# Ten instead of eight of the twelve d_ff blocks of tokens 768 to 1535 in seven-product steps, with a newly searched instruction order

## The chip, the core and the metric

The kernel runs on one NeuronCore of a Trainium2 chip. Its engines are TensorE (PE in the rows; PEld is its weight load), VectorE (DVE), ScalarE (ACT), GpSimd (POOL) and SyncE (SP), which issues every transfer here. The metric is the device time of one execution in microseconds.

## The reference

```python
# attention: B, H, S, D = 4, 8, 576, 64
scores = scale * q @ k.T ; causal mask ; a = softmax(scores)
local = a @ v
q_p = phi(q)                                   # elu(q) + 1
mem_out = (q_p @ M_prev) / (q_p . z_prev + 1e-6)
attn = g * mem_out + (1 - g) * local           # g = sigmoid(beta), one per head
x = attn.transpose(0, 2, 1, 3).reshape(2304, 512)
# gated MLP: w_a, w_b are 512 x 1536, w_out is 1536 x 512
out = (x @ w_a) * (x @ w_b) @ w_out
```

All is in float32, the MLP's weights arrive as float64. The kernel makes a product of two float32 matrices from three matmuls of float32r halves: high by high, high by low, low by high.

## The kernel before

**Stages.** The attention runs first, in sixteen pairs of heads, and fills the first 205 us; its outputs go to DRAM. Then comes the MLP. The 2304 tokens are six blocks of 384 (t = 0 to 5), d_ff is twelve blocks of 128 (f = 0 to 11). The weights are turned from float64 to two float32r halves while the MLP already runs, one block after another, by ScalarE, GpSimd and VectorE.

**Columns.** For t = 0 and 1 each (t, f) is a *column*: `half` makes a and b (12 matmuls of 384 token columns each, line 1027), `product` multiplies and splits them (ScalarE lines 1040 and 1047, VectorE lines 1043 and 300), `outer` adds the result times w_out to three output banks (9 matmuls of 512 columns, line 1064). There are 24 such columns. For t = 2 and 3 the blocks f from FA upward, here 8 to 11, are columns too, eight of them. The list `columns` is in lines 1501 to 1503.

**Seven-product steps.** The rest is done two token blocks at a time, by a scheme that needs seven 256 by 128 by 384 products where the two columns of a plain method need eight. A step n is one f for a pair of token blocks: n = 0 to 7 are f = 0 to 7 for t = 2 and 3 (group 0), n = 8 to 19 are all twelve f for t = 4 and 5 (group 1). A step

- loads the raw float32 weights of its f from DRAM into one of two buffers (`raw_load`, SyncE, line 1339), forms four differences of them on GpSimd (`raw_sums`, line 1354), and splits these (ScalarE line 1357, VectorE line 300);
- loads three ready split quarters (`whole_load`, line 1346);
- makes seven products of six matmuls (`part`, line 1381), with four copies on ScalarE (line 1396) and four joins on VectorE (line 1402) among them;
- splits the two hidden halves (lines 1417, 1419 and 300) and adds four rows of the output at once (`row`, 3 matmuls of 512 columns each, line 1433). Two more rows of each step are left for later: their split halves are kept in SBUF, at the place that `kept` gives, and `late_row` multiplies them once the group is over.

Before a group starts, its token blocks must be summed in eight pieces and split (VectorE line 1300, ScalarE line 1309).

**Memory units.** Tokens of t = 2 to 5 get their memory part in sixteen *units* (`memory_unit`), four for each t. A unit loads its q by four transfers of 48 KB (or eight of 24 KB), into one of two buffers; ScalarE's two exponentials of it (line 1182, 1183) wait for these transfers, VectorE normalises and turns it (the split of the turned tile, written `yl`, is the last reader of the buffer), TensorE multiplies it (line 1257), VectorE adds it to the attention's part.

**The order.** Each engine executes its instructions strictly in the order of one flat list, ORDER, of some 2900 names; BANKS gives the PSUM bank of each tile of the attention. A wait at the head of an engine's queue holds everything behind it.

Of the kernel before, what the change touches and what calls it, by code (L numbers as in the profile page):

```python
# [26 lines left out]
e4.0 e2A.1 lo1.0 m2B.1 r_.0 S_.1 n2.0 ma.2 H1.1 thq.2 m3B.1 m3A.1 mB.1 S_4.1 tlq.2 mb.2 n4.0 G5.0
Lk.3 mA.1 high1.1 G2B.0 n0.0 Lt.3 TQ.2 e2B.1 mx.0 e3B.1 n1.0 n3.0 e3A.1 shift2.0 ga.0 h2B.0 G4.0
m4.1 h5.0 G0.0 TK.2 eA.1 G3A.0 Lv.2 G1.0 l5.0 lo0.1 Lk.4 thQ.2 h4.0 h0.0 thK.2 h3A.0 w_0.0 eB.1
l2B.0 G2A.0 lo0.2 h2A.0 tlQ.2 clamp2.0 high1.2 low1.0 mu.2 G3B.0 l0.0 h3B.0 l4.0 e4.1 h1.0 b_3.2  # L30
tlK.2 S_3.2 TQ.3 thQ.3 Tq.3 l3A.0 shift2.1 l2A.0 l3B.0 TK.3 V1A.0 v_h.1 low1.1 m3A.2 l1.0 r_.1 thK.3
tlQ.3 e3A.2 V2A.0 ma.3 v_l.1 thq.3 b_2.2 xA.0 sq.4 tlK.3 mag0.2 n2.1 high2.1 S_2.2 mc.2 m3B.2 e3B.2
m2B.2 b_.2 mb.3 high1.3 S_.2 V1B.0 V2B.0 m2A.2 G2A.1 e2B.2 G2B.1 Lk.5 n4.1 mag1.4 n1.1 mB.2 tlq.3
e2A.2 G1.1 eB.2 clamp2.1 xB.0 md.2 h2A.1 mA.2 h2B.1 h1.1 n3.1 eA.2 n0.1 mu.3 l2A.1 S_4.2 mc.3 Lv.3
G0.1 G3B.1 m4.2 low2.2 l2B.1 h3B.1 G4.1 h0.1 v_h.2 TQ.4 l1.1 H1.2 h4.1 l3B.1 w_0.1 G3A.1 lo0.3 b_3.3
l4.1 h3A.1 shift0.1 shift0.2 e4.2 S_3.3 l3A.1 G5.1 r_.2 Lt.4 m3A.3 TK.4 l0.1 ma.4 h5.1 V1A.1 l5.1
thQ.4 v_l.2 m3B.3 lo1.1 V2A.1 thK.4 mag2.0 b_2.3 clamp1.1 tlK.4 tlQ.4 shift2.2 e3A.3 Lv.4 S_2.3
m2B.3 b_.3 m2A.3 n2.2 S_.3 sq.5 e3B.3 H0.0 n0.2 n1.2 mB.3 n3.2 xA.1 st_.0 e2B.3 mb.4 n4.2 e2A.3
V1B.1 high0.2 G0.2 eB.3 V2B.1 h0.2 clamp2.2 hi0.1 mag0.3 G2B.2 G2A.2 G5.2 xB.1 low2.3 h2A.2 Tq.4
G1.2 mA.3 w_0.2 mag0.4 h2B.2 md.3 mu.4 l2A.2 h1.2 S_4.3 l0.2 v_h.3 h5.2 G3B.2 thq.4 sq.6 G4.2 G3A.2  # L40
shift0.3 hl.0 b_3.4 l2B.2 l1.2 v_l.3 clamp2.3 l5.2 Lk.6 eA.3 S_3.4 h4.2 TK.5 tlq.4 me.2 m4.3 mag2.1
l4.2 hi1.0 TQ.5 shift1.3 hh.0 h3B.2 l3B.2 h3A.2 l3A.2 e4.3 mc.4 r_.3 V1A.2 thQ.5 m3A.4 n0.3 n4.3
Lt.5 b_2.4 tlQ.5 cx.1 m3B.4 thK.5 V2A.2 S_2.4 n2.3 Tq.5 n1.3 b_.4 lo0.4 tlK.5 S_.4 e3A.4 G0.3 ma.5
V1B.2 V2B.2 cx.2 xA.2 m2B.4 m2A.4 mb.5 e3B.4 hh.1 G2A.3 LM.2 thq.5 st_.1 G1.3 e2B.4 e2A.4 low1.2
high0.3 G5.3 G4.3 Lt.6 H0.1 h0.3 G2B.3 n3.3 lo1.2 mB.4 mA.4 eB.4 mag2.2 S_4.4 xB.2 tlq.5 h2A.3 H0.2
mu.5 TQ.6 shift0.4 h1.3 v_h.4 md.4 hl.1 high2.2 l2A.3 h5.3 G3A.3 h2B.3 b_3.5 h4.3 w_0.3 l0.3 l1.3
lo1.3 S_3.5 G3B.3 l5.3 v_l.4 eA.4 l2B.3 m4.4 h3A.3 TK.6 l4.3 V1A.3 e4.4 thQ.6 clamp1.2 mag2.3 mc.5
low0.2 mx.1 h3B.3 lo1.4 l3A.3 V2A.3 m3A.5 b_2.5 thK.6 r_.4 ma.6 me.3 e3A.5 low1.3 tlQ.6 n1.4 S_2.5
m3B.5 tlK.6 e3B.5 sq.7 b_.5 low0.3 hi1.1 l3B.3 S_.5 m2B.5 n0.4 mb.6 Tq.6 mB.5 hi0.2 n2.4 st_.2 Lt.7
# [1630 lines left out]
```

## Time and profile before

| | us |
|---|---|
| three runs | 652.19, 652.51, 655.13 (median 652.51) |
| the profiled execution, its own time | 654.46 |
| its span, first to last instruction | 652.7 |
| PE busy | 637.8 |
| DVE busy | 485.1 |
| ACT busy | 390.9 |
| POOL busy | 288.1 |

The time is 1.8 us more than the span. An engine is busy while an instruction of it executes; matmuls overlap in the record, so what the next costs is read from where it starts, not from its duration. The attention ends near 205 us, columns fill the time to about 400 us, seven-product steps the rest.

### The profile page before, as it was taken

The numbers are of one execution on the slowest core, as the hardware profiler recorded it, in microseconds if no ns is written. First come the engines' busy times: TensorE is split into PE (matmuls) and PEld (weight loads), VectorE is DVE, ScalarE is ACT, GpSimd is POOL, SyncE is SP. The second block draws the span as 40 slices with busy tenths as digits, with TensorE's granted clock in tenths as the row PEclk, the third lists the DMA queues.
The fourth block names the chain that finished last, engine by engine and source line by source line (L and its number), as shares of the span: only waits on it lengthen the run. The fifth ranks groups of instructions, "written<-read, shape, count | busy, mean of one in ns | idle before, by whom it ended". The sixth has DMA issues, their size and how long they took to land.

```text
span 652.7 us, 11644 instructions
## 1 busy us (share of the span) xinstructions
PE 637.8 (98%) x3962; PEld 586.1 (90%) x3962; DVE 485.1 (74%) x911; ACT 390.9 (60%) x941; POOL 288.1 (44%) x418
## 2 busy tenths in 40 slices
PE   8899999999999999999999999999989999999998
PEld 6788889999889899988999999999988999999987
DVE  7999998998889888889767679687758543545330
ACT  6999999999887445534555556556545433344220
POOL 4999999999995111461000006244140413233000
PEclk9999999999999999999999999999989999999999
DMA  7966776484763889987434436355733344525101
GB/s 175 197 138 166 189 155 168 121 190 136 231 202 138 281 280 323 313 273 267 125 69 97 113 107 202 102 155 172 219 74 113 129 125 149 166 93 161 49 33 64
DMA packets 142314, 105.43 MB, mean 162 GB/s; under 512 B 100272, under 2 KB 121776, under 8 KB 142256
## 3 DMA queue, kind: packets, MB, share of 16 engines
q1 hardware_dynamic: 142256, 104.70, 55.8%
q8 instruction: 31, 0.51, 0.3%
q14 instruction: 27, 0.22, 0.1%
HBM read 74.78 MB, written 29.88 MB: 160 GB/s over the span
## 4 chain that ended last, share of the span: by engine, by line
PE 71%; DVE 10%; DMA 5%; POOL 4%; ACT 4%; issue 2%; SPq 2%; ACTq 0%; DVEq 0%; POOLq 0%
PE pp L1381 20%; PE pp L1027 11%; PE pt L296 7%; PE o L1064 6%; PE o L1433 6%; PE pw L810 6%; PE pt L644 5%; PE pr L1433 4%; PE m L1433 2%; DVE wt L979 2%; DVE wt L986 1%; POOL P L710 1%; PE pw L644 1%; DMA q<-in_q_dram 1%; ACT P L693 1%
## 5 line engine op out<-in xcount | busy, mean ns | idle before, releaser
L1354 POOL TENSOR_TENSOR raw<-raw 128x256 f32<-128x256 f32 x80 | 67.3, 843 | 218.1 <-DMA raw<-ws 127.2
L710 POOL TENSOR_SCALAR P<-P,sum 128x128 f32<-128x128 f32 (+4 forms) x144 | 81.5, 587 | 2.5 <-DVE sum L702 2.2
L693 ACT ACTIVATE P<-pt,nm 128x384 f32<-128x384 f32 (+3 forms) x128 | 66.9, 535 | 2.8 <-DVE nm L683 1.4
L300 DVE TENSOR_TENSOR PT<-pt,PT 128x512 fp32r<-128x512 f32 (+2 forms) x112 | 61.8, 586 | 4.0 <-ACT PT L765 2.9
L810 PE MATMUL pw<-PT,vh 128*128 128x448 f32 (+4 forms) x352 | 61.0, 316 | 0.4 <-ACT xo L819 0.3
L683 DVE TENSOR_REDUCE nm<-pt 128x1 f32<-128x128 f32 (+3 forms) x128 | 56.3, 480 | 4.6 <-PE pt L644 3.9
L810 PEld LDWEIGHTS pw<-PT,vh 128*128 128x128 f32 x352 | 54.9, 189 | 4.5 <-ACT xo L819 0.6
L296 PE MATMUL pt<-ident,P 128*128 128x128 f32 (+1 forms) x400 | 55.2, 277 | 1.3 <-POOL P L710 0.7
L1027 PE MATMUL pp<-xh,abh 128*128 128x384 f32 x160 | 53.9, 337 | 1.6 <-ACT x L1040 1.0
L765 ACT ACTIVATE PT<-pt 128x512 fp32r<-128x512 f32 (+2 forms) x112 | 53.3, 527 | 3.5 <-PE pw L810 2.0
L1027 PE MATMUL pp<-xh,abl 128*128 128x384 f32 x160 | 53.8, 336 | 0.0
L1027 PE MATMUL pp<-xl,abh 128*128 128x384 f32 x160 | 53.6, 335 | 0.0
L965 POOL TENSOR_SCALAR wt<-wt 128x512 f32<-128x512 f32 (+1 forms) x21 | 19.9, 949 | 66.9 <-ACT wt L959 66.8
L296 PEld LDWEIGHTS pt<-ident,P 128*128 128x128 f32 (+1 forms) x400 | 44.1, 140 | 5.2 <-POOL P L710 1.6
L1402 DVE TENSOR_TENSOR u<-pp,u 128x384 f32<-128x384 f32 x40 | 22.2, 555 | 35.0 <-PE pp L1381 28.3
L1381 PE MATMUL pp<-xh,abh 128*128 128x384 f32 x112 | 37.7, 336 | 1.9 <-ACT h L1396 1.9
L1381 PE MATMUL pp<-xh,abl 128*128 128x384 f32 x112 | 37.9, 339 | 0.0
L1064 PE MATMUL o<-wh,hl 128*128 128x512 f32 x96 | 37.8, 394 | 0.0
L1381 PE MATMUL pp<-xl,abh 128*128 128x384 f32 x112 | 37.8, 337 | 0.0
L1064 PE MATMUL o<-wl,hh 128*128 128x512 f32 x96 | 37.8, 393 | 0.0
L1064 PE MATMUL o<-wh,hh 128*128 128x512 f32 x96 | 37.4, 389 | 0.0
L959 ACT ACTIVATE wt<-wr 128x1024 f32<-128x1024 f32 (+1 forms) x24 | 22.0, 917 | 23.9 <-DMA ws<-wt 9.7
(248 smaller groups left out, 1925.6 us busy)
## 6 DMA issues: line engine op xcount, KB each, us to landing
raw<-ws SPq DMA_DIRECT2D x20, 512.0 KB, 4.4
xs<-xo SPq DMA_DIRECT2D x16, 576.0 KB, 4.4
abh<-wsa SPq DMA_DIRECT2D x18, 384.0 KB, 3.4
abl<-wsa SPq DMA_DIRECT2D x18, 384.0 KB, 4.2
wr<-in_moe_w_a_dram SPq DMA_DIRECT2D x12, 512.0 KB, 5.3
wr<-in_moe_w_b_dram SPq DMA_DIRECT2D x12, 512.0 KB, 6.1
wr<-in_moe_w_out_dram SPq DMA_DIRECT2D x12, 512.0 KB, 4.4
ws<-wt SPq DMA_DIRECT2D x12, 512.0 KB, 3.1
```

What stands on the lines that cost most here:

```text
L296: nc.tensor.transpose(out, x, ident[0:x.shape[0], 0:x.shape[0]])
L300: eng.tensor_tensor(out=lo, in0=x, in1=hi, op=ALU.subtract)
L683: nc.vector.tensor_reduce(out=s["nm"][:, c:c + 1], in_=src, axis=AX.X, op=ALU.min)
L693: nc.scalar.activation(out=s["P", i][:, h, :], in_=src, func=AF.Exp, scale=-1.0, bias=s["nm"][:, c:c + 1], accum_out=s["sums"][:, c, 0:1],)
L710: nc.gpsimd.tensor_scalar(out=pr[:, h, :], in0=pr[:, h, :], scalar1=r[:, c:c + 1], scalar2=1.0, op0=ALU.mult, op1=ALU.mult,)
L765: nc.scalar.activation(out=dst, in_=src, func=AF.Copy)
L810: nc.tensor.matmul(pv[:, a:hi], lhsT=w, rhs=x, start=(n == 0), stop=(n == len(ops) - 1))
L1027: nc.tensor.matmul(pp, lhsT=w[:, w0:w0 + P], rhs=x[:, kk, :], start=(c == 0), stop=(c == 3 * KK - 1),)
L1064: nc.tensor.matmul(po[t, m], lhsT=hx[:, m * P:(m + 1) * P], rhs=w, start=(f == START_F[t] and n == 0), stop=(f == NFT - 1 and n == 2 and t ...
L1354: nc.gpsimd.tensor_tensor(out=o, in0=x, in1=y, op=op)
L1381: nc.tensor.matmul(r[nm], lhsT=a[:, kk * P:(kk + 1) * P], rhs=b[:, kk, :], start=first and c == 0, stop=True, skip_group_check=True,)
L1433: nc.tensor.matmul(o, lhsT=hx[:, a:a + P], rhs=z, start=bool(first and i == 0), stop=last and i == 2, skip_group_check=True,)
```

## The change

FA goes from 8 to 10. Blocks f = 8 and 9 of t = 2 and 3 leave the columns (28 instead of 32 remain) and become two more steps of group 0, which has ten steps then; group 1 follows as n = 10 to 21. `kept` gets a place for the kept halves of the two new steps: the fourth quarter of the two regions into which `whole_load` writes, where group 1 keeps its own first two. ORDER and BANKS are replaced as a whole, in the attention too.

```diff
 ORDER = """
-Dk.0 id.0 Dq.0 zi.0 ib.0 clamp1.0 ms.0 wm.14 TK.0 low2.0 Dk.1 mk.0 thK.0 TQ.0 b_2.0 thQ.0 Dq.1 zq.0
...
+id.0 high0.1 zi.0 wm.14 low2.0 Dk.0 TK.0 mag0.2 Dq.0 thK.0 Dk.1 mk.0 zq.0 TQ.0 Ek.0 high1.0 thQ.0 Dq.1
...
-    FA = 8
+    FA = 10
     START_F = {0: 0, 1: 0, NB: FA, NB + 1: FA}
...
                 return [x.rearrange("p k c -> p (k c)")[:, (f - 2) * Q:(f - 1) * Q] for x in xhl[1]]
+        elif f > 7 and not g:
+            a = W6 * (f - 6) + 3 * Q
         else:
             a = W6 * 4 + (f - 4 * g) * Q
```

**ScalarE, the last memory unit.** `ph<-q` and `ph<-ph` are the exponentials of a unit, `n<-n` and `yh<-q` belong to the units too; `u`, `h` and `pp` out of `pp` are the copies of a step, `hh` and `abh` out of `u` or `h` its splits, `abh<-raw` the split of its weight differences. Before:

```order
L1419 ACTIVATE abh<-h_6507 128x256
L1247 ACTIVATE m<-xx 128x384
L1396 ACTIVATE u_6609<-pp 128x384
L1417 ACTIVATE hh<-u_6540 128x384
L1182 ACTIVATE ph<-q_6626 128x384
L1183 ACTIVATE ph<-ph 128x384
L1396 ACTIVATE h_6640<-pp 128x384
L1396 ACTIVATE u_6642<-pp 128x384
```

Now:

```order
L1361 ACTIVATE abh<-raw_4391 128x1024
L1214 ACTIVATE n_6472<-n_6470 32x12 x4
L1421 ACTIVATE hh<-h_6427 128x128
L1423 ACTIVATE abh<-h_6427 128x256
L1400 ACTIVATE u_6533<-pp 128x384
L1400 ACTIVATE h_6544<-pp 128x384
L1421 ACTIVATE hh<-u_6438 128x384
L1400 ACTIVATE u_6574<-pp 128x384
L1242 ACTIVATE yh<-q_6347 128x384
L1184 ACTIVATE ph<-q_6507 128x384
L1185 ACTIVATE ph<-ph 128x384
L1400 ACTIVATE pp<-pp 128x384
```

Behind the unit's exponentials two copies of a step stood before; now the split of another unit and three copies have moved ahead of them, and the copy right behind is that of the next step.

**SyncE, the transfers around the last load of q.** `abh` and `abl` out of `wsa` are the split quarters, `raw` out of `ws` the raw weights. Before:

```order
L1339 DMA raw_4391<-ws_61 128x1024
L1346 DMA abh<-wsa_80 128x768
L1346 DMA abl<-wsa_80 128x768
L1157 DMA q_6626<-in_q_dram 32x12x32 x4
L1176 DMA xf<-xs 64x384
```

Now:

```order
L1343 DMA raw_4392<-ws_70 128x1024
L1350 DMA abh<-wsa_81 128x768
L1350 DMA abl<-wsa_81 128x768
L1159 DMA q_6507<-in_q_dram 32x12x32 x4
L1178 DMA xf<-xs 64x384
```

The load stands behind the same kinds of transfers as before; they now belong to the two blocks that have become steps.

**VectorE, the pieces ahead of the first step.** `pc...` out of `xf` and `xl` out of `xf` are splits of the eight pieces, `xf<-xf` their sums, `x` and `hl` belong to columns. Before:

```order
L1078 COPY raw_4391<-o_5475 128x512
L300 TENSOR_TENSOR pcT1l<-xf,pcT1h 128x768
L1300 TENSOR_TENSOR xf<-xf 128x768 x2
L1218 TENSOR_TENSOR n_5624<-n_5623,n_5625 128x12
L1221 TENSOR_SCALAR n_5624<-n_5624,over_gate_91 128x12
L1225 RECIPROCAL n_5624<-n_5624 128x12
L1043 TENSOR_TENSOR x<-pp,x 128x384
L1230 TENSOR_TENSOR ph<-ph,n_5624 128x384
L1300 TENSOR_TENSOR xf<-xf 128x768
```

Now:

```order
L302 TENSOR_TENSOR xl_98<-xf,xh_97 128x768
L302 TENSOR_TENSOR pcT1l<-xf,pcT1h 128x768
L1302 TENSOR_TENSOR xf<-xf 128x768 x3
L302 TENSOR_TENSOR pcTT2l<-xf,pcTT2h 128x768
L302 TENSOR_TENSOR pcT4l<-xf,pcT4h 128x768
L1045 TENSOR_TENSOR x<-pp,x 128x384
L1206 TENSOR_REDUCE n_5614<-q_5441 128x12
```

The sums and splits, which stood between parts of columns and units, now stand together.

## Rows read from the trace of the kernel before

**Rows 1.** The page, busy time of each engine.
```profile
PE 637.8 (98%) x3962; PEld 586.1 (90%) x3962; DVE 485.1 (74%) x911; ACT 390.9 (60%) x941; POOL 288.1 (44%) x418
```

**Rows 2.** Stretches: us; busy of PE, PEld, DVE, ACT, POOL (x instructions); clock; DMA.
```profile
0.00:50.00 50.00, 46.07 (x362) 38.27 (x363) 44.51 (x103) 42.85 (x123) 39.67 (x68) 1.00 0.80 174
...
100.00:150.00 50.00, 50.00 (x429) 45.86 (x429) 44.41 (x97) 47.35 (x137) 48.52 (x83) 1.00 0.66 158
150.00:200.00 50.00, 47.95 (x391) 42.88 (x389) 42.83 (x88) 44.01 (x119) 47.39 (x74) 1.00 0.58 180
200.00:250.00 50.00, 48.74 (x264) 45.83 (x263) 44.04 (x59) 24.96 (x38) 11.28 (x12) 1.00 0.75 255
250.00:300.00 50.00, 47.80 (x251) 44.07 (x250) 43.34 (x54) 23.52 (x35) 19.83 (x22) 1.00 0.92 294
...
350.00:400.00 50.00, 50.00 (x269) 47.35 (x268) 39.12 (x75) 28.43 (x64) 4.40 (x6) 1.00 0.46 132
...
450.00:500.00 50.00, 48.13 (x245) 44.43 (x244) 36.62 (x70) 25.96 (x58) 12.79 (x15) 0.97 0.44 117
```

**Rows 3.** Waits of PE, whole span: total us, times, longest us.
```profile
PE pp L1027 <- ACT x L1040: 2.4, 3, 1.0
...
PE pp L1381 <- ACT h L1396: 1.9, 1, 1.9
...
PE pp L1027 <- DVE x L1043: 1.1, 2, 0.6
```

**Rows 4.** Chain and ACT's timeline near 478 us: start, us, what [idle before].
```profile
471.92 5.72 DMA q<-in_q_dram
...
477.74 0.52 ACT L1182 ACTIVATE ph<-q 128x384 f32<-128x384 f32 x1 [3.69 <-DMA q<-in_q_dram]
...
478.73 0.48 ACT h L1396
479.25 1.59 PE pp L1381 x6
```

**Rows 5.** PE's timeline behind that stop: start us, us, instruction [idle before].
```profile
479.25 0.44 PE L1381 MATMUL pp<-xh,abh 128*128 128x384 f32 x1 [1.87 <-ACT h L1396]
...
480.64 0.63 PE L1433 MATMUL o<-wh,hh 128*128 128x512 f32 x1
481.06 0.63 PE L1433 MATMUL o<-wl,hh 128*128 128x512 f32 x1
...
484.41 0.39 PE L1433 MATMUL o<-wh,hh 128*128 128x512 f32 x1
```

**Rows 6.** Transfers into q, from issue to landing.
```profile
DMA to landing us min/median/max: 1.6/2.2/6.5
```

**Rows 7.** Runs of matmuls in the chain: start us, us, what.
```profile
318.95 8.34 PE pp L1027 x48
...
510.00 4.18 PE pp L1381 x24
...
631.28 8.17 PE pr L1433 x36
```

**Rows 8.** Groups by shape, 205 to 640 us (POOL: whole span): busy us, mean ns.
```profile
L300 DVE TENSOR_TENSOR abl<-raw,abh 128x1024 fp32r<-128x1024 f32 x20 | 25.8, 1289 | 7.6 <-ACT abh L1357 7.6
L1402 DVE TENSOR_TENSOR u<-pp,u 128x384 f32<-128x384 f32 x40 | 22.2, 555 | 35.0 <-PE pp L1381 28.3 <-ACT u L1396 6.7
L300 DVE TENSOR_TENSOR hl<-x,hh 128x384 fp32r<-128x384 f32 x31 | 20.0, 644 | 3.7 <-ACT hh L1047 2.9
L1043 DVE TENSOR_TENSOR x<-pp,x 128x384 f32<-128x384 f32 x31 | 17.1, 550 | 10.8 <-ACT x L1040 6.3 <-PE pp L1027 4.1 <-ACT pcT3h L1309 0.5
...
L300 DVE TENSOR_TENSOR hl<-u,hh 128x128 fp32r<-128x128 f32 x12 | 3.5, 290 | 3.2 <-ACT hh L1417 3.2
...
L1354 POOL TENSOR_TENSOR raw<-raw 128x256 f32<-128x256 f32 x80 | 67.3, 843 | 218.1 <-DMA raw<-ws 127.2 <-ACT pcT3h L1309 86.2
```

**Rows 9.** L1354's durations (ns, min/median/max), and DVE's timeline while it runs.
```profile
L1354 POOL TENSOR_TENSOR raw<-raw x80: 727/740/1605, 395.3 to 599.2; 128x256 f32<-128x256 f32 x80
...
471.70 0.83 DVE L300 TENSOR_TENSOR hl<-h,hh 128x128 fp32r<-128x128 f32 x1
```

More of the change, by code (lines that the diff above doesn't have):

```diff
@@ L27 @@
[L27 to L49, printed above, removed]
@@ new lines @@
+Lv.9 b_2.9 hi1.5 pb.8 e3A.9 Lv.10 S_2.9 n4.8 tlQ.10 thK.10 high1.7 b_.9 pc.8 H0.7 m3B.9 st_.6
+shift0.8 Lp.10 S_.9 clamp0.8 V1B.7 m2A.9 V2B.7 Tq.10 G5.8 xA.7 clamp2.7 lo1.7 m2B.9 hi1.6 e3B.9
+H1.10 clamp0.9 n3.8 clamp1.6 mB.9 e2A.9 hi1.7 shift2.6 n0.8 hl.3 e2B.9 pe.8 Lk.12 G4.8 eB.9 v_l.8
+thq.10 xB.7 H0.8 h5.8 mA.9 n1.8 low1.6 G2A.8 tlK.10 shift1.6 G0.8 h4.8 S_4.9 h2A.8 v_h.9 G1.8
+high0.8 px.7 tlq.10 h0.8 G2B.8 low2.9 pf.8 hi0.9 l5.8 clamp0.10 pd.9 eA.9 G3B.8 w_0.8 h1.8 b_3.10
+clamp2.8 l4.8 m4.9 l2A.8 mag1.8 l1.8 h2B.8 S_3.10 h3B.8 Lk.13 G3A.8 l2B.8 sq.12 pa.9 TK.11 shift2.7
@@ new lines @@
+Kload.23 uo.14 Kshift.22 uhh.15 uB.16 uA.16 Ksplit_keep.20 Khigh.22 Klow.22 Khi.22 ucx.16 uhl.15
+Klo.21 Kmag.23 Klo.22 Kkeep.22 umx.16 Kclamp.23 Kshift.23 uB.17 Khigh.23 Klow.23 Khi.23 Klo.23
+Ksplit_keep.22 uA.17 wo.0 uhh.16 q_phi.0 ucx.17 uhl.16 q_phi2.0 q_norm.0 q_load.1 q_norm2.0
+q_x_load.1 q_pairs.0 umx.17 q_over_norm.0 q_norm3.0 q_turn.0 uo.15 uo.16 uhh.17 uhl.17 q_turn_h.0
+q_turn_l.0 uB.18 uo.17 q_load.2 q_phi.1 q_phi2.1 q_norm.1 ucx.18 q_norm2.1 ua.0 q_x_load.2 uA.18
+q_pairs.1 q_seed.0 q_over_norm.1 uc.0 uA.19 q_phi.2 umx.18 q_load.3 q_retrieve.0 q_norm3.1 q_turn.1
@@ new lines @@
+q_turn_h.1 uhh.18 q_join.0 q_phi2.2 q_turn_l.1 q_norm.2 uA.20 q_norm2.2 uB.19 q_seed.1 uhl.18
+q_pairs.2 ub.0 q_retrieve.1 ucx.19 uo.18 q_over_norm.2 q_norm3.2 q_turn.2 q_turn_h.2 q_x_load.3
+q_phi.3 umx.19 uB.20 q_turn_l.2 uB.21 q_seed.2 uhh.19 q_load.4 q_join.1 sh.0 q_phi2.3 q_norm.3
+q_retrieve.2 q_norm2.3 q_x_load.4 uhl.19 q_pairs.3 q_over_norm.3 q_norm3.3 q_join.2 uA.21 q_load.5
+uo.19 ucx.20 q_seed.3 q_turn.3 q_turn_h.3 q_phi.4 umx.20 uhh.20 q_turn_l.3 q_phi2.4 q_retrieve.3
+q_norm.4 q_norm2.4 q_pairs.4 q_seed.4 ucx.21 wl.1 q_join.3 uhl.20 q_phi.5 q_over_norm.4 q_norm3.4
@@ new lines @@
+q_turn.4 sl.0 uA.22 uo.20 umx.21 q_turn_h.4 q_phi2.5 uhh.21 q_turn_l.4 uB.23 q_norm.5 q_load.6
+q_norm2.5 sh.1 q_pairs.5 q_x_load.5 uB.22 uA.23 q_retrieve.4 uhl.21 ucx.22 q_over_norm.5 umx.22
+uhh.22 ucx.23 q_norm3.5 q_phi.6 uhl.22 q_turn.5 umx.23 q_phi2.6 q_norm.6 uhh.23 uo.21 uo.22
+q_x_load.6 q_norm2.6 q_turn_h.5 uhl.23 q_join.4 q_pairs.6 uo.23 q_turn_l.5 ua.1 q_load.7 q_seed.5
+q_over_norm.6 sl.1 q_norm3.6 q_retrieve.5 q_join.5 uc.1 q_x_load.7 q_turn.6 q_turn_h.6 q_turn_l.6
+uB.24 sh.2 sl.2 ucx.24 uA.24 umx.24 uhh.24 yal.0 ub.1 p2.0 uA.25 co.4 q_phi.7 q_phi2.7 q_norm.7
@@ new lines @@
+q_norm2.7 q_load.8 Ml.3 q_seed.6 q_pairs.7 q_retrieve.6 q_join.6 uhl.24 q_over_norm.7 uB.25
+q_norm3.7 q_seed.7 q_turn.7 cp1.0 uo.24 ucx.25 q_turn_h.7 umx.25 uhh.25 q_turn_l.7 q_phi.8
+q_retrieve.7 uhl.25 uo.25 Mp.3 q_join.7 pw.0 sh.3 q_phi2.8 pw.1 sh.4 q_norm.8 pw.2 sl.3 yal2.0 sl.4
+ch1.0 rl.0 uB.26 co.5 sh.5 co.6 ru.0 ucx.26 uA.26 co.7 sh.6 sl.5 sl.6 sh.7 q_x_load.8 umx.26 yal.1
+uhh.26 rl.1 q_norm2.8 q_pairs.8 uB.27 ucx.27 uA.27 uhl.26 uo.26 rh.0 q_load.9 q_over_norm.8 q_seed.8
+q_norm3.8 q_turn.8 rs.0 ybe.0 umx.27 q_turn_h.8 q_turn_l.8 sl.7 q_load.10 rl.2 cu2.0 q_x_load.9
@@ L225 @@
+2354025340125320510125401542031201435435205432105341251304134205413024153142510342510435132
 """
```

349 lines of the change are left out of this document (172 added, 177 removed).

## The prediction

> **What bounds the kernel now.** I read the busy times first: TensorE is busy 98% of the span, the next engine 74% [rows 1]. A share over 650 us hides stages, so I went to the stretches next [rows 2]. In the attention, 100 to 150 us, TensorE has no idle time, and GpSimd, ScalarE and VectorE are busy 48.5, 47.4 and 44.4 of 50 us: four engines are full together. From 200 to 300 us, where the weights are turned, VectorE is the fullest beside it (44.0 and 43.3 of 50), and TensorE loses 1.3 and 2.2 us. From 350 to 400 us TensorE is full and VectorE at 39.1. In 450 to 500 us TensorE loses 1.9 us and its mean clock is 0.97.
>
> The list of TensorE's waits says what these losses are [rows 3]: 3.5 us for ScalarE and VectorE in columns, and one single stop of 1.9 us in the steps. The chain shows the origin of the latter [rows 4]: a transfer of q for the last memory unit, issued at 471.92, took 5.72 us against a median of 2.2 [rows 6]. ScalarE stood 3.69 us at the unit's exponential, and a step's copy was queued behind it; TensorE needed that copy. The stop costs more than itself. [...] From 479.25 to 484.41 stand 12 matmuls of 384 and 6 of 512 columns, 5.16 us; at the full pace (8.34 us for 48 and 4.18 for 24 of 384 columns, so 0.174 each [rows 7]) they take 12 x 0.174 + 6 x 0.227 = 3.45. The stop is worth 1.87 + 1.71 = 3.6 us in this execution.
>
> **The change part by part.**
>
> *The matmuls.* A pair of columns has 2 x 24 products of 384 columns, a step 7 x 6 = 42. The outer part is equal, 18 matmuls of 512 either way (two columns of nine; four rows at once and two late rows of three each). Two pairs go, two steps come: 12 matmuls less, 12 x 0.174 = **2.09 us**. TensorE is the full engine from 300 us on, so this comes off the end in full.
>
> *Work added elsewhere.* VectorE loses, for each of the four columns, 0.550 + 0.644 us, and gains for each step a split of 1.289, four joins of about 0.56 and the splits of the hidden halves, about 1.5 in sum [rows 8]: 2 x 5.0 - 4 x 1.2 = +5.2 us. GpSimd gains 8 subtractions of 0.843, 6.7 us. ScalarE gains about as much as VectorE, by its copies and splits of like sizes; SyncE gains two raw loads and four loads of split quarters. Spread over the 250 us of steps all this is nothing: VectorE's fullest stretch from 350 us on has 11 us free in 50, and GpSimd is the idlest engine there [rows 2]. What matters is where it is put.
>
> *The entry to the steps.* With four columns gone, the first step begins 20 us earlier on TensorE's own count of work, while the sixteen units' work is moved up by only 7 to 14 us. I counted VectorE's instructions in the new order over 60 us of TensorE's work from column 21's outer products on, and the same stretch in the old one. New are two more raw splits (1.289), eight joins (0.56), four hidden splits (about 0.65), about one more unit's share (some seven operations of 0.55 to 0.65), less six or so operations of columns and pieces: 2.6 + 4.5 + 2.6 + 4.2 - 4 = about 10 us. Before, VectorE was busy 39.1 of 50 there [rows 2], 47 of 60; now it is 57 of 60. No stretch of the old trace has VectorE so full beside columns. The nearest are 200 to 300 us, at 87 to 88%, where TensorE lost 1.3 and 2.2 us in 50: over 60 us that is 1.5 to 2.7. The lower bound is zero, since a unit's work is needed late and may trail; the upper is 2.7 with the clock's part on top as at the stop (3.6 for 1.87), so about 5. I take **1.5**, the lower of the two nearest rows, because the four columns that are left as cover stand in the middle of it.
>
> *The late transfer.* The last unit's load waits for the split that last reads its buffer, and for the quarters ahead of it in SyncE's queue. From the later of these to the exponential there were about 6.8 us of TensorE's work in the old order, and there are 8.9 in the new: 2 us more, against a stop of 1.87. The same landing would leave ScalarE waiting some 1.6 us and TensorE not at all. So **-3.6** is taken as gone. But the unit two before it now has only 3.7 us between release and exponential, so the stop can come again there; that is a rival below.
>
> *The added wait.* Blocks 8 and 9 keep their late halves where group 1 keeps its first two, so ScalarE's split of step 10 must wait until TensorE's late rows have read block 8. In the new order that row ends 1.4 us of matmuls ahead of the split, block 9's 3.1 us ahead of step 11's. Behind the split on ScalarE stand copies of step 11, for which TensorE waits. I cost it at nothing, since TensorE is the full engine there and reaches the row in its turn; if it were 1 us late, 1 us would be the price.
>
> *The new order of the attention.* Each pair of heads has the same instructions. Where four engines are full nothing is to be won; room is at both ends, 3.9 us in 0 to 50 and 2.1 in 150 to 200 [rows 2]. So at most 6 is won, and as much may be lost; nothing shows the sign and I take zero, with half of either way in the range.
>
> *The sum,* from the profiled execution's 654.46: - 2.09 - 3.6 + 1.5 = **650.3**. This execution is 1.95 above the median of 652.51; if most of that is the stop, whose size hangs on one landing, a median run holds 1.6 of it, and 652.51 - 2.09 - 1.6 + 1.5 is 650.3 as well.
>
> [...] While GpSimd's subtractions ran, one VectorE split of 128x128 took 0.83 us [rows 9]; its like takes 0.290 in the mean [rows 8]. [...]
>
> **The rivals.**
>
> *The late landing stays a cost.* The unit with 3.7 us, or another, stops ScalarE before a copy as before. For it: the longest landing is 6.5 us [rows 6], and four issues of about half a microsecond precede it. Against it: the copies needed soonest stand ahead of that exponential now. Then 3.6 is not won, and part of the 1.5 is the same stop: 654.46 - 2.09 + 0 to 1.5 = 652.4 to 653.9, say 653.
>
> *Nothing is lost at the entry,* and the attention's ends tighten a little: 654.46 - 5.7 = 648.8 down to 645.8 with half of the 6. For it: columns need only blocks 10 and 11 now, so the first loads of split quarters no longer wait for columns of blocks 8 and 9. Say 647.9.
>
> *Slower: VectorE becomes the bound at the entry.* About twelve of GpSimd's subtractions fall into the 60 us. If each holds up a VectorE split by the 0.54 us seen once, or by its own 0.74, that is 6.5 to 8.9 us; on 57 of 60 it makes 63.5 to 66, 3.5 to 6 over. TensorE stops for these, and the clock falls with each longer stop (3.6 for 1.87): 7 to 11.5. The time is 654.46 - 5.7 + 7 to 11.5 = 656 to 660, say 658. It decides for slower from about 3.7 us of overrun. For it: the full stretch. Against it: the median of the subtractions, and VectorE's idle time before the stretch.
>
> **How the numbers follow.** Chances: forecast 0.42, late landing stays 0.26, nothing lost 0.20, VectorE bound 0.12. Half a percent, about what a measurement of this kernel can tell, is 3.3 us: faster means below 649.2, slower above 655.8. Faster is the 0.20 and the lower part of the forecast's spread (0.13): 0.33. Slower is the 0.12. The rest, 0.55, is the same. The forecast's own range is 648.8 to 652.5. To hold 8 in 10 the range takes in the late landing with its upper end and most of "nothing lost": 647.3 to 654.6; left out are the slow rival and the last part of the attention's gain.
>
> **What would show it.** Counts: products of columns fall by 96 matmuls, those of steps rise by 84. The wait of ScalarE's exponential for q: gone or under 2 us without a stop of TensorE is the forecast; a stop with 0.42 us between matmuls behind it is the late landing. Between 350 and 420 us: TensorE idle by 1 to 2 us with VectorE over 90% busy is the forecast, 4 us or more the slow rival, with splits of 0.29 us stretched beside the differences. The attention's end tells its part: near 205 us as before, or 3 either way. Wrong would be the whole argument if TensorE stopped in the late steps, behind 500 us, where it never waits now.

## The result and the profile after

The changed kernel takes **656.77 us** in the median (653.36 to 662.0, 16 runs), the kernel before 652.05 on the same chip (650.8 to 655.13, 16 runs): a ratio of **1.0083, interval 1.0056 to 1.0111**, slower by 0.8%. The forecast was 650.3 with a range of 647.3 to 654.6. The ratios and intervals of this document are worked out from fast executions alone, so they can differ a little from the quotient of two medians. The profiled execution took 662.0, at the slow end of its runs; a second one, below, took 659.04.

Busy time of each engine, from the page of the kernel after, against [rows 1]:

```profile
PE 640.1 (97%) x3950; PEld 584.6 (89%) x3950; DVE 504.3 (76%) x919; ACT 393.8 (60%) x949; POOL 300.2 (45%) x426
```

The 12 matmuls less are there (3962 before). VectorE is busy for 19 us more and GpSimd for 12, where the added work was put at 5.2 and 6.7: instructions took longer, as shown below. Nothing in this line says that the kernel is slower. The stretches do, as in [rows 2] (us; busy time of PE, PEld, DVE, ACT, POOL with the count of instructions; granted clock; DMA), with one of 50 to 100 us:

```profile
50.00:100.00 50.00, 44.29 (x366) 38.56 (x365) 49.30 (x98) 42.79 (x124) 47.71 (x74) 1.00 0.56 148
...
350.00:400.00 50.00, 49.10 (x256) 45.02 (x255) 43.13 (x80) 29.27 (x68) 10.20 (x10) 1.00 0.45 126
400.00:450.00 50.00, 49.64 (x276) 46.77 (x275) 42.47 (x82) 29.87 (x72) 19.19 (x23) 1.00 0.70 182
450.00:500.00 50.00, 49.64 (x263) 46.47 (x262) 36.93 (x70) 27.45 (x64) 18.18 (x20) 1.00 0.46 135
```

In the trace of before the first of these stretches reads:

```profile
50.00:100.00 50.00, 49.65 (x426) 44.34 (x425) 48.39 (x110) 48.47 (x139) 48.52 (x77) 1.00 0.71 174
```

TensorE loses 5.7 us in 50 where it lost 0.35, and the stretch holds 366 of its matmuls instead of 426. VectorE is busier (49.3 us) with fewer instructions (98 for 110): some took longer. The time is gone in the attention, in the middle of it. The late steps, where I had placed the risk, lose 0.9, 0.4 and 0.4 us.

TensorE's waits, against [rows 3] (total us, times, longest us), and under them one line of the same list of the kernel before:

```profile
PE pt L298 <- DVE PT L302: 5.7, 2, 4.0
PE pp L1029 <- ACT x L1042: 2.4, 3, 1.4
...
PE pp L1029 <- DVE x L1045: 1.1, 2, 0.9
...
PE pt L296 <- DVE PT L300: 2.0, 3, 1.4
```

The stop of 1.9 us for a step's copy behind the last unit's load is gone. The waits for VectorE's copies of PT, 2.0 us in three before, are two stops now, 5.7 us in all. VectorE's timeline of the kernel after (start us, us, instruction) shows what these copies stood behind:

```profile
80.75 1.67 DVE L394 SCALAR_TENSOR_TENSOR rn<-rn,over_gate 128x8 f32<-128x8 f32 x1
...
91.65 0.68 DVE L393 TENSOR_REDUCE rn<-qr 128x8 f32<-128x512 f32 x1
92.36 5.53 DVE L394 SCALAR_TENSOR_TENSOR rn<-rn,over_gate 128x8 f32<-128x8 f32 x1
97.93 0.20 DVE L397 RECIPROCAL rn<-rn 128x8 f32<-128x8 f32 x1
...
98.54 2.05 DVE L302 TENSOR_TENSOR PT<-pt,PT 128x384 fp32r<-128x384 f32 x4
```

L394, the instruction that adds 1e-6 to a tile's norms and multiplies them by the gate, handles eight numbers a partition. It has six executions, one for each token tile of the memory part; in the kernel before they took 0.17 to 0.32 us. Here two of them took 1.67 and 5.53. GpSimd, at the same time, worked without a pause (its timeline, kernel after):

```profile
87.88 4.81 POOL L712 TENSOR_SCALAR P<-P,sum 128x384 f32<-128x384 f32 x9 [1.37 <-DVE sum L704]
92.65 1.00 POOL L434 TENSOR_TENSOR xx<-xx 128x384 f32<-128x384 f32 x1
93.63 0.41 POOL L779 TENSOR_SCALAR PT<-P 128x256 fp32r<-128x256 f32 x1
...
95.53 1.26 POOL L302 TENSOR_TENSOR vh<-vr,vh 128x512 fp32r<-128x512 f32 x1
...
98.03 1.27 POOL L302 TENSOR_TENSOR vh<-vr,vh 128x512 fp32r<-128x512 f32 x1
```

In the kernel before the same instruction for the same tile stood 2.5 us earlier, in the middle of GpSimd's nine divisions of P, and passed (VectorE's timeline, and the one line of GpSimd's under it):

```profile
89.84 0.29 DVE L392 SCALAR_TENSOR_TENSOR rn<-rn,over_gate 128x8 f32<-128x8 f32 x1
...
86.03 4.81 POOL L710 TENSOR_SCALAR P<-P,sum 128x128 f32<-128x128 f32 x9
```

The stop it makes, and the five microseconds behind it, from TensorE's timeline and the stretches of the kernel after:

```profile
99.14 1.57 PE L298 MATMUL pt<-ident,P 128*128 128x128 f32 x8 [3.95 <-DVE PT L302]
...
100.00:105.00 5.00, 5.00 (x30) 3.97 (x29) 4.28 (x7) 3.04 (x7) 0.00 (x0) 0.70 0.10 23
```

After 3.95 us of waiting, TensorE's granted clock is 0.70 in the mean of five microseconds: it was 0.50 from 99.60 to 103.01 us and 1.00 behind. That is some 1.5 us more.

The traces divide cleanly into two parts, the attention (up to the start of its last product with PT) and what comes after it (up to the last matmul's end). Each line is one profiled execution. The median is that of the executions of that run, and the ratio compares them with executions of the kernel before beside them, whose median was 652.05 beside the kernel after and 651.69 beside the last three.

| kernel | profiled us | attention us | second part us | median us, ratio to before (interval) |
|---|---|---|---|---|
| before | 654.46 | 205.2 | 444.2 | 652.05 |
| before, again | 650.36 | 204.0 | 441.4 | (one run) |
| after | 662.0 | 213.7 | 443.4 | 656.77, 1.0083 (1.0056 to 1.0111) |
| after, again | 659.04 | 209.4 | 444.8 | 661.83, 1.0134 (1.0102 to 1.0165) |
| old attention, new steps | 651.97 | 205.2 | 441.5 | 652.6, 1.0013 (0.9995 to 1.0032) |
| new attention, old steps | 660.53 | 213.3 | 442.1 | 657.89, 1.0100 (1.0064 to 1.0136) |

### The profile page after: what moved, and what is told of

Its sections match the earlier page's. It is cut to its first block, busy times and chain, and to the rows that moved or that the text cites. A ratio compares the mean times of both kernels' runs of the same rounds, so it can differ in the third digit from the quotient of the medians.

```text
span 660.2 us, 11671 instructions
## 1 busy us (share of the span) xinstructions
PE 640.1 (97%) x3950; PEld 584.6 (89%) x3950; DVE 504.3 (76%) x919; ACT 393.8 (60%) x949; POOL 300.2 (45%) x426
## 4 chain that ended last, share of the span: by engine, by line
PE 71%; DVE 14%; DMA 7%; ACT 3%; issue 3%; SPq 2%; POOL 1%; DVEq 0%; ACTq 0%; POOLq 0%
PE pp L1385 20%; PE pp L1029 10%; PE pt L298 8%; PE o L1437 6%; PE pw L812 6%; PE pt L646 6%; PE o L1066 5%; PE pr L1437 5%; PE m L1437 2%; DMA raw<-ws 2%; DVE PT L302 2%; PE pw L646 2%; DVE wt L988 2%; DVE nm L685 1%; DVE wt L981 1%
## 5 line engine op out<-in xcount | busy, mean ns | idle before, releaser
L1358 POOL TENSOR_TENSOR raw<-raw 128x256 f32<-128x256 f32 x88 | 78.2, 889 | 146.1 <-DMA raw<-ws 140.9
L712 POOL TENSOR_SCALAR P<-P,sum 128x384 f32<-128x384 f32 (+4 forms) x144 | 82.3, 593 | 12.0 <-ACT xo L821 7.0
L298 PE MATMUL pt<-ident,P 128*128 128x128 f32 (+1 forms) x400 | 56.9, 279 | 7.0 <-DVE PT L302 5.7
L1406 DVE TENSOR_TENSOR u<-pp,u 128x384 f32<-128x384 f32 x44 | 24.3, 551 | 40.4 <-PE pp L1385 25.2
L967 POOL TENSOR_SCALAR wt<-wt 128x512 f32<-128x512 f32 (+1 forms) x21 | 19.9, 946 | 70.6 <-ACT wt L961 66.4
L1400 ACT ACTIVATE u<-pp 128x384 f32<-128x384 f32 x44 | 21.6, 491 | 50.7 <-PE pp L1385 33.5
L1029 PE MATMUL pp<-xh,abh 128*128 128x384 f32 x128 | 44.3, 346 | 3.3 <-ACT x L1042 2.2
L1029 PE MATMUL pp<-xh,abl 128*128 128x384 f32 x128 | 43.8, 342 | 0.3 <-DVE abl L302 0.3
L1029 PE MATMUL pp<-xl,abh 128*128 128x384 f32 x128 | 43.6, 340 | 0.0
L1385 PE MATMUL pp<-xh,abl 128*128 128x384 f32 x124 | 41.8, 337 | 0.4 <-DMA abl<-wsa 0.4
L1385 PE MATMUL pp<-xh,abh 128*128 128x384 f32 x124 | 41.6, 336 | 0.4 <-ACT pp L1400 0.4
L1385 PE MATMUL pp<-xl,abh 128*128 128x384 f32 x124 | 41.8, 337 | 0.0
L335 POOL TENSOR_SCALAR md<-mr 64x256 fp32r<-64x256 f32 x10 | 5.4, 536 | 68.0 <-DMA mr<-in_M_prev_dram 67.4
L1066 PE MATMUL o<-wh,hl 128*128 128x512 f32 x84 | 33.3, 396 | 0.0
```

The costliest lines, as they stand in the source:

```text
L298: nc.tensor.transpose(out, x, ident[0:x.shape[0], 0:x.shape[0]])
L712: nc.gpsimd.tensor_scalar(out=pr[:, h, :], in0=pr[:, h, :], scalar1=r[:, c:c + 1], scalar2=1.0, op0=ALU.mult, op1=ALU.mult,)
L1029: nc.tensor.matmul(pp, lhsT=w[:, w0:w0 + P], rhs=x[:, kk, :], start=(c == 0), stop=(c == 3 * KK - 1),)
L1066: nc.tensor.matmul(po[t, m], lhsT=hx[:, m * P:(m + 1) * P], rhs=w, start=(f == START_F[t] and n == 0), stop=(f == NFT - 1 and n == 2 and t ...
L1358: nc.gpsimd.tensor_tensor(out=o, in0=x, in1=y, op=op)
L1385: nc.tensor.matmul(r[nm], lhsT=a[:, kk * P:(kk + 1) * P], rhs=b[:, kk, :], start=first and c == 0, stop=True, skip_group_check=True,)
```

## The experiments

**Which half loses the time.** My theory from these rows (A): the loss lies in the new attention order. Rival (B): it lies in the new steps, or in the way the two meet. The order list holds the same items up to its item pp.0 in both kernels, so the halves can be exchanged.

```diff
 # e1_old_attention: the kernel after, with
-ORDER = <order of after up to pp.0> <order of after from pp.0>, BANKS of after
+ORDER = <order of before up to pp.0> <order of after from pp.0>, BANKS of before
 # e2_new_attention: the kernel before, with
-ORDER = <order of before up to pp.0> <order of before from pp.0>, BANKS of before
+ORDER = <order of after up to pp.0> <order of before from pp.0>, BANKS of after
```

> The changed kernel with the old order and banks up to the end of the attention (both lists hold the same instructions there) and the new order behind it, FA = 10. Theory A, the loss lies in the new order of the attention, whose last product came at 213.7 us instead of 205.2 in the profiled execution, while the MLP behind it took 0.85 us less: 649.5 to 651.5 us, last attention product near 205. Theory B, the loss lies in the steps and columns (a fuller VectorE at the entry): 655 to 657, last attention product near 205. Theory C, the loss lies where the two meet: about 653 to 654.

> The kernel before with the new order and banks in the attention alone, FA = 8. Theory A (attention): 656 to 658 us, with two long VectorE instructions near 81 and 92 us and the last attention product past 207. Theory B (steps): 651.5 to 652.5. Theory C: about 654.

The old attention with the new steps gave 652.6 us, 1.0013 (0.9995 to 1.0032). The new attention with the old steps gave 657.89, 1.0100 (1.0064 to 1.0136). Theory A holds: the whole loss goes with the attention order. The long instructions went with it too, in the old kernel otherwise (VectorE's timeline of the new attention with the old steps):

```profile
80.14 1.68 DVE L392 SCALAR_TENSOR_TENSOR rn<-rn,over_gate 128x8 f32<-128x8 f32 x1
...
91.76 5.56 DVE L392 SCALAR_TENSOR_TENSOR rn<-rn,over_gate 128x8 f32<-128x8 f32 x1
```

And the steps by themselves win nothing either; that is taken up below.

**Is it the second input?** L394 reads two tensors from SBUF. One reading (A1) was that the second input makes it wait, and that without it the loss is gone. This kernel takes that input away; the memory part of tokens 0 to 767 is then scaled by a constant.

```diff
-            nc.vector.scalar_tensor_tensor(
-                out=rn2, in0=rn2, scalar=1e-6, in1=over_gate, op0=ALU.add, op1=ALU.mult
-            )
+            nc.vector.tensor_scalar(
+                out=rn2, in0=rn2, scalar1=1e-6, scalar2=2.0, op0=ALU.add, op1=ALU.mult
+            )
```

> The changed kernel, but the instruction that adds 1e-6 to a tile's norms and multiplies them by the gate multiplies by a constant instead of by a second tile, so it reads one input from SBUF (the memory part of tokens 0 to 767 is scaled wrongly, six instructions of 128x8 differ). In the profiled execution two of them took 1.67 and 5.53 us instead of 0.2. Theory A1, VectorE waits there because of its second SBUF input while GpSimd works without a pause: all six at 0.3 us or less, time 651 to 654, no run above 657. Theory A2, the attention's order is slow for another reason: time 655.5 to 658, runs at 660 and above again.

It gave 661.7 us (653.09 to 665.23), 1.0104 (1.0069 to 1.0138). A1 falls: the time stays, and the one-input form waits as long in the first place (VectorE's timeline of this kernel):

```profile
79.68 1.67 DVE L394 TENSOR_SCALAR rn<-rn 128x8 f32<-128x8 f32 x1
```

Its profiled execution happens to be its fastest, with 0.37 us at the second place. The spread of 12 us fits this: in one kernel the same instruction sometimes waits and sometimes doesn't, as the next profile shows.

**The kernel after once more,** unchanged.

> The changed kernel itself, for a second profile beside the others. Theory A1: if this execution lies near 662, one of the six norm instructions takes over 4 us again; if it lies near 654 to 657, none does. Theory B: the attention's end is the same in both and the difference lies behind it.

It gave 661.83 us. At the first place L394 took 1.67 us as before; at the second 0.17, since it came 1.3 us later and met a pause of GpSimd (VectorE's and GpSimd's timelines of this execution):

```profile
93.66 0.17 DVE L394 SCALAR_TENSOR_TENSOR rn<-rn,over_gate 128x8 f32<-128x8 f32 x1
...
92.71 1.02 POOL L434 TENSOR_TENSOR xx<-xx 128x384 f32<-128x384 f32 x1
94.81 0.41 POOL L779 TENSOR_SCALAR PT<-P 128x256 fp32r<-128x256 f32 x1 [1.08 <-ACT P L767]
```

So this execution's attention ended at 209.4 and not at 213.7. What it had saved there it lost partly in the second part (444.8), where TensorE stopped for 1.49 us at 312 us. More on this below.

**The small instructions moved, both ways.** If the place of these three instructions decides (A2), taking them out of GpSimd's unbroken runs should give the time back, and putting one into such a run should cost it in the old kernel. The rival (A3): the new order has too little room there in any case.

```diff
 # e4_md_moved: order of after, the three instructions of rn for tiles 6 and 7 (items md.6, md.7)
-... n1.5 h3B.4 n2.5 ...            ... sq.8 md.6 cx.2 ...
+... n1.5 h3B.4 md.6 n2.5 ...       ... sq.8 cx.2 ...
-... mx.5 m3B.7 high1.5 ...         ... shift2.5 md.7 mA.7 ...
+... mx.5 m3B.7 md.7 high1.5 ...    ... shift2.5 mA.7 ...
 # e5_md7_late: order of before
-Lp.7 md.7 n4.6 tlK.8 l2A.6
+Lp.7 n4.6 tlK.8 md.7 l2A.6
```

> The kernel after with two small pieces of VectorE work standing elsewhere: the three instructions that make rn for token tiles 6 and 7 (L393, L394, L397) are issued earlier, while GpSimd works through the eight or nine one-input divisions of P (L712), instead of while it works through products and subtractions of two tensors. Nothing else moves and the output is the same. Theory A2 (a VectorE instruction with all operands in SBUF, however small, is held up by GpSimd's back-to-back instructions, and these two hold-ups of 1.67 and 5.53 us are what the new attention order loses): L394 under 0.4 us in all eight places, no 4 us wait of TensorE for PT, last attention product at 205 to 207 us, and a median 5 us below the kernel after: 651 to 654, and hardly an execution above 657. Rival A3 (the long L394 is a symptom; the new order has too little slack between scores, VectorE and products, and loses the time in any case): 656 to 661, another wait of some us for PT between 78 and 110 us, and executions above 660 as often as in the kernel after (about half).

> The kernel before with a single change of place: the three VectorE instructions that make rn for token tile 7 (L391, L392, L395) stand one instruction later, behind the subtraction f<-pt,f of 0.64 us instead of ahead of it. So L392 would start at about 91.6 us, where GpSimd begins six subtractions and sums of two tensors nearly without a pause (91.66 to 96.71), instead of at 89.84 beside its divisions of P. The order on the other engines is the same. Theory A2: L392 grows from 0.29 to between 1.5 and 5.5 us, VectorE's copies of PT behind it come as much later, TensorE waits 1 to 4 us for them near 93 to 100 us, and the median is 1 to 5 us above the kernel before (653 to 657). Rival A3 (the place of such a small instruction doesn't decide, the slack of the order does): L392 may grow, but the time stays within 0.5 us of the kernel before, since the old order has the room.

The second is the plainest run of the study. Three instructions change places with one, on one engine, and the order on all others is the same: **654.59 us against 651.34, 1.0040 (1.0017 to 1.0063)**. VectorE's timeline of this kernel, and under it GpSimd's and TensorE's:

```profile
90.37 0.68 DVE L391 TENSOR_REDUCE rn<-qr 128x8 f32<-128x512 f32 x1
91.08 3.32 DVE L392 SCALAR_TENSOR_TENSOR rn<-rn,over_gate 128x8 f32<-128x8 f32 x1
94.44 0.20 DVE L395 RECIPROCAL rn<-rn 128x8 f32<-128x8 f32 x1
...
93.97 0.42 POOL L777 TENSOR_SCALAR PT<-P 128x256 fp32r<-128x256 f32 x1
94.47 0.72 POOL L300 TENSOR_TENSOR PT<-P,PT 128x256 fp32r<-128x256 f32 x1
...
95.12 2.18 PE L296 MATMUL pt<-ident,P 128*128 128x128 f32 x9 [2.48 <-DVE PT L300]
```

L392 ends at 94.40, in the first gap that GpSimd leaves (0.08 us, from 94.39 to 94.47); the five changes of instruction before that, which follow each other without one, didn't let it in. TensorE then waits 2.48 us for PT, and its granted clock falls, to 0.50 in the mean of the five microseconds of this stretch and 0.85 in the next five. That costs this execution more than the wait, some 2.5 us and 0.75:

```profile
95.00:100.00 5.00, 4.88 (x22) 3.83 (x23) 4.62 (x9) 2.48 (x7) 3.37 (x6) 0.50 1.10 266
```

A3's bet, that the old order has the room, is wrong.

The first gave 654.35 us, 1.0046 (1.0028 to 1.0065), and none of its 12 runs is above 658.1, where the kernel after reached 664. That is about half of the loss or more, but not all: 651 to 654 was expected. L394 now took 0.50 and 0.33 us, where under 0.4 was expected. But I had put these instructions ahead of the subtraction f, which TensorE needs (VectorE's, then TensorE's timeline):

```profile
88.23 0.33 DVE L394 SCALAR_TENSOR_TENSOR rn<-rn,over_gate 128x8 f32<-128x8 f32 x1
...
88.71 0.64 DVE L304 SCALAR_TENSOR_TENSOR f<-pt,f 128x512 fp32r<-128x512 f32 x1
...
75.24 0.22 PE L646 MATMUL pt<-mask,ident_b 128*128 128x128 bf16 x1 [1.07 <-DVE f L304]
...
89.41 0.38 PE L646 MATMUL pt<-mask,ident_b 128*128 128x128 bf16 x4 [0.86 <-DVE f L304]
```

**The same, one to two instructions later,** behind f.

```diff
 # e6_md_moved_2: order of after
-... n1.5 h3B.4 n2.5 ... V1B.4 l3B.4 m3B.6 ...       (md.6, md.7 taken out of their old places)
+... n1.5 h3B.4 n2.5 ... V1B.4 l3B.4 md.6 m3B.6 ...
-... sq.9 tlQ.8 S_2.7 ...
+... sq.9 tlQ.8 md.7 S_2.7 ...
```

> As the run with the three instructions of rn for token tiles 6 and 7 placed earlier, but each again one to two VectorE instructions later there: behind the subtraction f<-pt,f (L304) and the copy of PT instead of ahead of them. In that run these 1.3 us stood ahead of f, for which TensorE then waited 1.07 and 0.86 us (its two new gaps of 1.24 and 1.03 us at 73.9 and 88.3 us). Theory A2 (the hold-ups of these small instructions are all that the new attention order loses): no gap of TensorE over 0.6 us between 50 and 110 us, last attention product at 205 to 206.5 us, median 652 to 653.5, which is what the old attention order gave with these steps (652.6). Rival A3 (the new order also has less room around 75 to 100 us, whatever stands there): another gap of about 1 us in that stretch, last attention product at 207 or later, and 654 to 655.5 as before this second move.

It gave 654.87 us, 1.0054 (1.0035 to 1.0073): no better. The gaps for f are gone, but others of 0.6 to 1.4 us stand at 26, 78, 80, 93 and 173 us, and the attention ends at 209.1 in this execution. So A3 has a part as well. Against executions of the kernel before, the kernel after loses 0.8 and 1.3% in its two runs, the moved orders 0.5%, the old attention with the same steps 0.1%. So the two small instructions make 2.5 to 6 us, and some 2 to 3 us belong to the new order beside them. These lie in the same place. Matched matmul by matmul, the orders are level up to 72 us: the 89th product with PT starts at 72.4 us in the kernel before, at 72.8 in the kernel after and at 72.3 and 72.5 with the instructions moved. The 133rd starts at 95.2, 103.9, 98.1 and 98.4. Which instruction makes the 2 to 3 us there, these runs don't show.

**The late transfer and the steps.** A second profile of the kernel before asks whether its stop of 1.87 us is usual.

> A second profile of the kernel before, to see whether the stop of 1.87 us at the last unit's late q transfer and the 1.71 us of low clock behind it belong to its usual execution. If the stop is usual: again 652 to 655 with a wait of ScalarE for q of 1 us or more near 478 us and a stretch from the last attention product to the last product of the kernel of about 444.2 us. If it is one execution's: 650 to 652, no such wait or under 0.6 us, and that stretch 440.5 to 442.5 us, so that the stop was never worth 3.6 us in the median.

Its size is not. ScalarE waited again for the landing, but TensorE only 0.55 us (ScalarE's and TensorE's timelines of this execution):

```profile
475.39 0.53 ACT L1182 ACTIVATE ph<-q 128x384 f32<-128x384 f32 x1 [2.37 <-DMA q<-in_q_dram]
...
476.90 0.44 PE L1381 MATMUL pp<-xh,abh 128*128 128x384 f32 x1 [0.55 <-ACT h L1396]
```

The stop itself is usual, though. The other two profiles of the old steps have it too: 0.59 us at 487 us with the new attention, 1.31 at 484 with the one change of place. Over the four executions it has a mean of 1.1 us, and a low clock (0.50 from 480.14 to 483.55 us) stood behind it in one alone.

The second part of this execution takes 441.4 us, against 444.2 in the profile that I argued from and 441.5 with the new steps. So the new steps, free of that stop and 2.09 us of matmuls shorter, are no faster than the old. What ate the gain are new waits at the entry and in the steps. I added up, matmul by matmul, the time between two starts beyond what is usual for the shape: from 375 to 500 us it is 4.7 us with the new steps and 2.2 in the second profile of the kernel before, 2.5 us more, against 2.09 won. TensorE's list for the old attention with the new steps:

```profile
PE pp L1029 <- ACT x L1042: 1.6, 2, 1.0
PE pp L1029 <- DVE x L1045: 1.5, 2, 1.1
...
PE pp L1385 <- DMA abl<-wsa: 1.1, 1, 1.1
```

The large ones stand at 306, 382 and 464 us. The first belongs to the turning of the weights and has its like in the kernel before; the other two, at the entry and for a landing of abl, are new. Each had a cause in the order of single instructions. I took them away, first one and then all three.

```diff
 # e7_old_attention_x_first: e1, at the entry to the steps
-... sl.5 sl.6 sh.7 q_x_load.8 umx.26 ...        (sl.6: pcT4l<-xf,pcT4h; umx.26: x<-pp,x)
+... sl.5 umx.26 sl.6 sh.7 q_x_load.8 ...
 # e8_three_moves: e7, and
-... Khigh.21 Klow.21 Khi.21 umx.15 ...          (Klow.21: L988)
+... Khigh.21 umx.15 Klow.21 Khi.21 ...
-... sl.5 umx.26 sl.6 sh.7 ... q_turn.8 rs.0 ybe.0 ...      (rs.0: abl<-raw,abh)
+... sl.5 umx.26 sh.7 ... q_turn.8 rs.0 sl.6 ybe.0 ...
-... or3.5 rl.9 or2.5 ybe.7 wl.8 ...             (rl.9: load of raw; wl.8: loads of abh, abl)
+... or3.5 wl.8 rl.9 or2.5 ybe.7 ...
```

> The kernel after with the old attention order (the run that gave 652.6), and one VectorE instruction more moved: at the entry to the seven-product steps the product x<-pp,x (L1045) stands ahead of the subtraction pcT4l<-xf,pcT4h (1.49 us beside GpSimd's sums of the weights) instead of behind it. TensorE waited 1.1 us for that x at 382 us, of its three waits of about 1.1 us in the second part. If the new waits at the entry are what eats the 2.09 us of matmuls that the change takes away, each can be had back one by one: the wait falls to 0.2 to 0.6 us and the median to 651.6 to 652.4. Rival: the wait only moves to the next instruction of VectorE, which has no free time there (its 24 of 25 us are full), and the time stays at 652.3 to 653.

> The kernel after with the old attention order and x<-pp,x ahead of pcT4l (the run that gave 651.5), and three more moves against the three waits of TensorE of about 1.1 us that its trace still shows in the second part. At 305.8 us: the product x<-pp,x (L1045) stands ahead of L988 on VectorE, so that GpSimd's clamp of the next weights (L967, 1.09 us) runs beside an instruction that reads PSUM and not beside L988, which took 1.41 us there for 0.69. At 386.3 us: the subtraction pcT4l (1.49 us) stands behind the halves of the weights' sums (L302 abl<-raw) that TensorE waited 0.9 us for. At 463.3 us: the loads of abh and abl (L1350) are issued ahead of the load of raw (L1343), which waits for its buffer until 456.8 us, instead of behind it; TensorE waited 1.1 us for abl. Theory (what eats the gain of the change in the second part are single waits made by the places of single instructions): the three gaps fall to 0.2 to 0.6 us each, the second part from 440.8 to 438.5 to 440, the median to 649 to 650.5, below the kernel before (ratio 0.996 to 0.999). Rival (VectorE has no free time there, and another instruction is late next): two of the gaps stay near 1 us, and the median is 651 to 652.

One move: 651.54 us, 1.0006 (0.9986 to 1.0025), not clear of the run without it. The wait at 382 us went, but one of 1.06 us for abl came 4 us later: the rival's picture, with a little left over. All moves: **650.17 us against 651.74, 0.9979 (0.9966 to 0.9992)**, with a second part of 439.7. This version beats both kernels, the one before by 0.2%. The three further moves were run together, so what each is worth by itself isn't shown. The first of them shows best how it works. VectorE's L988 and GpSimd's clamp L967, with one move and then with all:

```profile
300.44 1.41 DVE L988 SCALAR_TENSOR_TENSOR wt<-wr,wt 128x512 uint32<-128x512 uint32 x1
301.77 0.54 DVE L1045 TENSOR_TENSOR x<-pp,x 128x384 f32<-128x384 f32 x1
...
300.21 1.09 POOL L967 TENSOR_SCALAR wt<-wt 128x1024 f32<-128x1024 f32 x1 [1.28 <-ACT wt L961]
```

```profile
301.23 0.56 DVE L1045 TENSOR_TENSOR x<-pp,x 128x384 f32<-128x384 f32 x1
301.71 0.82 DVE L988 SCALAR_TENSOR_TENSOR wt<-wr,wt 128x512 uint32<-128x512 uint32 x1
...
300.90 1.08 POOL L967 TENSOR_SCALAR wt<-wt 128x1024 f32<-128x1024 f32 x1 [1.29 <-ACT wt L961]
```

The clamp now runs beside x<-pp,x, whose input pp lies in PSUM and which takes its usual 0.55 us; L988 comes behind and is 0.6 us shorter. TensorE's wait behind this, with one move and with all:

```profile
306.96 0.44 PE L1029 MATMUL pp<-xh,abh 128*128 128x384 f32 x1 [0.86 <-ACT x L1042]
```

```profile
307.17 0.45 PE L1029 MATMUL pp<-xh,abh 128*128 128x384 f32 x1 [0.37 <-ACT x L1042]
```

The wait for abl at 463 us is gone, and the one at the entry is split into two gaps of 0.50 and 0.53 us, which together are as long as before.

## Why the prediction was wrong, point by point

**The matmuls, -2.09: right.** 3962 became 3950: the products of columns fell from 768 to 672, those of steps rose from 840 to 924. By count this is 2.09 us of TensorE's own work. That it comes off the end in full was not borne out: TensorE is not full between 350 and 500 us any more, and with the old attention the new steps gave 1.0013.

**The added work, +5.2 us of VectorE: too small.** With the old attention order VectorE is busy for 498.3 us, 13.2 more than before. Set against the usual length of each form, its instructions behind 206 us were held up for 22.6 us there and 16.0 in the kernel before (counting those over 0.15 us). These 6.6 us are most of the 8.0 that the term missed. TensorE had to wait for little of it.

**The late transfer, -3.6: the mechanism is right, the size that of one execution.** The stop at the last unit is absent from all profiles with the new steps. In the four with the old steps it is 0.55 to 1.87 us; with the one low clock of 1.71 us (3.41 us at 0.50) this makes 1.5 us in the mean, near the 1.6 that I took as the median's share and far from 3.6. The rival named with it, that the stop comes again at an earlier unit, came true in part. It is 0.36 and 0.34 us long in the two profiles of the kernel after, and 1.15 with the small instructions moved, behind the load of the twelfth unit (ScalarE's and TensorE's timelines of that kernel):

```profile
421.03 0.52 ACT L1184 ACTIVATE ph<-q 128x384 f32<-128x384 f32 x1 [3.08 <-DMA q<-in_q_dram]
...
422.54 0.44 PE L1385 MATMUL pp<-xh,abh 128*128 128x384 f32 x1 [1.15 <-ACT pp L1400]
```

**The entry, +1.5: about right, but a second wait of its size was not in the sum.** With the old attention and the new steps TensorE loses 2.5 us more than in the second profile of before between 375 and 500 us, where the kernel before has its 0.55 for the late landing; so about 3 us are new, twice the forecast and inside its bounds of 0 and 5. Half of it is a wait at the entry for VectorE, as forecast; the other half is a landing again, of abl, which I had not considered. TensorE waits for it in all seven profiles with the new steps in which its load stands behind that of raw (0.4 to 1.1 us), and not in the one in which the load was moved. With all four moves 1.8 us of the second part came back, 0.5 of it at 306 us.

**The added wait of the kept halves, 0: right as far as seen.** No list of TensorE's waits names it.

**The new order of the attention, 0 with 6 either way: this step failed.** It was argued from counts: the same instructions in each pair, four engines full in the middle, room only at the ends, so nothing to win in the middle and the sign open. Nothing was won, but something can be lost where four engines are full, and it isn't made up there: the kernel after is 8.7 us behind at the 133rd product with PT and 8.3 at the 331st. The loss was 5 to 10 us, at 72 to 105 us. What I compared was the amount of work in a stretch. What decided is which VectorE instruction stood beside which GpSimd instruction, and this can be read from the two orders: GpSimd is busy 48.5 of 50 us there in the row of before above, so almost any VectorE instruction meets it, and of those that read two inputs from SBUF beside a working GpSimd 501 of 1,227 were held up by over 0.15 us. The bound of 6, taken from the idle time at both ends, bounds a gain. It says nothing of a loss. What the runs showed in place of the zero is 1.0% for the new order alone, some 6.5 us, and moving two small instructions gave 2.5 to 6 us back.

**The slower rival had the right mechanism in the wrong place.** It had VectorE held up by GpSimd, 656 to 660, with a chance of 0.12, at the entry to the steps alone. There, from 350 to 450 us, VectorE was held up for 6.5 to 8.5 us in the two profiles of the kernel after and the one with the old attention (5 before), each instruction by at most 0.6, and TensorE lost 1 to 2 us. In the attention, where GpSimd is busy some three times as densely (47.7 of 50 us from 50 to 100 us in the kernel after, against 10.2 and 19.2 from 350 to 450), it was not asked. Nor was its price right: a hold-up was taken as 0.54 to 0.74 us, the length of one GpSimd instruction, and two of them took 1.4 and 5.3 beyond their usual length. Most hold-ups outlasted no more than one instruction of GpSimd: of the 501 instructions with two SBUF inputs that were over 0.15 us longer than usual, 480 saw no more than one GpSimd instruction end while they ran, L394 of the moved kernel at 0.33 us among them. That of L394 in the kernel after is not of this kind: in its 5.53 us nine instructions of GpSimd ended.

## What to carry to other kernels

When two orders of the same instructions are compared, counts and busy shares don't tell them apart: list the VectorE instructions that take two inputs from SBUF (here 501 of 1,227 beside a working GpSimd were held up by over 0.15 us), or are a tensor_scalar or a cast from it (59 were), see what GpSimd does beside each, and give those that stand in an unbroken run of GpSimd a price of up to several of its instructions (nine of them ended here in the 5.53 us of L394). Put them beside GpSimd's pauses, and let instructions that read PSUM (none of 4,081 was held up by over 0.02 us), and reductions (none of them by over 0.15), fill the time in which GpSimd is busy. And take further profiles of the kernel before, ahead of pricing a stop that one late landing made: here it was 0.55 to 1.87 us.
